# Spectral filter, expert layer and MLP in one kernel: first and last transform in pairs of chunks, x before the other loads, constant tables on SyncE's queue

## The chip, the cores and the metric

One core of a Trainium2 chip runs the whole program. The metric is the device time of one execution in microseconds (us). A difference counts here as one over 0.2% of the time before, 6.7 us.

## The reference

```python
X = np.fft.rfft(x, axis=1)                       # x: 8 x 3072 x 256
Yr = X.real @ w_r - X.imag @ w_i + b_r
Yi = X.real @ w_i + X.imag @ w_r + b_i
Y  = shrink(Yr, 0.01) + 1j * shrink(Yi, 0.01)    # soft threshold
x  = np.fft.irfft(Y, n=3072, axis=1).reshape(24576, 256)
# 8 experts, the best one per token, tokens with x @ w_skip > 0 only
out = x;  out[t] += gate[t] * relu(x[t] @ w1[e]) @ w2[e]
h = out @ w_in
y = (max(h, 0) + alpha * min(h, 0)) @ w_out      # d_ff = 2048
```

## The kernel before, in words

The 3072-point transform of a batch is split in two. Token index and frequency are cut as 3072 = 48 x 64, so the work of one batch b (of 8) has four stages.

- **A** (`A_load` L163, `A_mm` L179, `A_store` L184): the 48-point part, over all 64 residues m. A residue is (j, q) with j in 0, 1 and q in 0..31. The 32 q are cut into 8 *chunks* of 4. A chunk is loaded by two DMAs (one for each j) to an `xin` tile of 48 partitions twice, each partition getting 4 rows of 256 numbers, 4 KB in one run. `quarters` (L169) does eight matmuls, ScalarE copies one half out of PSUM and VectorE the other (L177), and two DMAs store the tile `sa` to the DRAM scratch `sA`.
- **B and C** (`S_load`, `B_mm`, `mix`, `gather`, `shrink`, `C_mm`, `C_store`): the 64-point part, by 24 residue classes taken in 12 pairs `pp`. `S_load` fetches six classes (three pairs) from `sA`; it needs all chunks of the batch stored. `B_mm` multiplies by the class matrices `fct` (L215, L235), `mix` applies the weights (L292 for pair 0, L263 for the others), `C_mm` turns back with the matrices `cct` (L330, L324), and ScalarE copies the result to a tile `zc` (L331, L325, L326), of which there are two. `C_store` (L335) writes it to the scratch `sZ`.
- **D** (`D_load` L339, `D_mm` L345, `D_store` L350): the 48-point part backwards, again in 8 chunks: `zin` in, `xo` out, and the rows of the filtered tokens go to the DRAM buffer `xb`, 2 rows (2 KB) to a run. `T_tr` transposes `xo` for the router.
- Then routing, expert jobs and the MLP (L882 to L1067), which read `xb`.

The order is written by hand. A loop over steps s = 12 b + pp (L707) does in each step: stores that are due (`store`, the `zc` store first), x loads for the chunks of step s + 2 (`a_need`), D loads for step s + 2 (`d_need`), every third step an `S_load`, then `B_mm` of the next pair, `mix`, a D chunk, `C_mm` of the pair before, and the A chunks of the step. `a_at` (L573) says how many half chunks (units u) of A a step gets: two (one chunk) up to step 14 and in the steps with s % 12 in 0, 1, 2, 11; one in the others. So batch b + 1 goes through A while batch b goes through B and C.

Before the loop, batch 0 goes through A alone: 8 chunks, `setup0` (L630, it makes the weight tables `wri` on VectorE) after the sixth. Then the first `S_load`, cut into three DMAs of two classes, and B starts (L215).

Nearly all DMAs are issued by SyncE (SP in the profile) in program order: an instruction that waits keeps everything behind it waiting. The 8 tables `fct` and `cct` (six classes each) are issued by GpSimd, and in batch 0 the second half of each A store by ScalarE. The framework gives SP's and ScalarE's DMAs eight completion semaphores in turn, so a DMA also waits until the last one on its own semaphore has landed.

Of the kernel before, what the change touches and what calls it, by code (L numbers as in the profile page):

```python
# [10 lines left out]
F32 = mybir.dt.float32  # L11
# [9 lines left out]
B, SEQ, D = 8, 3072, 256  # L21
NT = B * SEQ
NQ, NP = 32, 96
NC = 24
# [18 lines left out]
CP = 6  # L43
# [4 lines left out]
def _constants():  # L48
    A, G = np.zeros((2, 64, 64)), np.zeros((2, 64, 64))
    n1 = np.arange(48)  # L50
    for c in range(NC):
        ang = 2 * np.pi * ((n1 * c) % 48) / 48
        for ri in range(2):
            if c == 0:
                f = g = np.ones(48) if ri == 0 else (-1.0) ** n1
            else:
                f = np.cos(ang) if ri == 0 else -np.sin(ang)
                g = 2 * f
            A[:, :48, 2 * c + ri] = f
            G[:, 2 * c + ri, :48] = g / SEQ  # L60
    Fm, Cm = np.zeros((NC, 128, 128)), np.zeros((NC, 128, 128))
    n2 = np.arange(64)
    for c in range(NC):
        for f in range(64):
            if c:
                k = c + 48 * f
                rows, sg, mul = None, (1 if f < 32 else -1), 1
            else:
                k = 24 * (f // 32) + 48 * (f % 32)
                rows, sg, mul = slice(64 * (f // 32), 64 * (f // 32) + 64), 1, 2  # L70
            ang = 2 * np.pi * ((n2 * k) % SEQ) / SEQ
            co, si = np.cos(ang), np.sin(ang)
            if c:
                Fm[c, :64, f], Fm[c, 64:, f] = co, si
                Fm[c, :64, 64 + f], Fm[c, 64:, 64 + f] = -si * sg, co * sg
                Cm[c, f, :64], Cm[c, f, 64:] = co, si
                Cm[c, 64 + f, :64], Cm[c, 64 + f, 64:] = -si * sg, co * sg
            else:
                Fm[0, rows, f], Fm[0, rows, 64 + f] = co, -si
                Cm[0, f, rows], Cm[0, 64 + f, rows] = mul * co, -mul * si  # L80
                if f == 0:
                    Fm[0, rows, 64] = np.cos(np.pi * n2)
                    Cm[0, 0, rows] = 1.0
                    Cm[0, 64, rows] = np.cos(np.pi * n2)
    m = np.arange(64)
    m = 32 * (m // 2 % 2) + 4 * (m // 8) + 2 * (m // 4 % 2) + m % 2
# [9 lines left out]
    q = 16 * (r // 12) + 4 * g + 2 * (c // 48 % 2) + c // 96 % 2  # L96
# [12 lines left out]
def spectral_moe_mlp(ctx, tc, x, w_r, w_i, b_r, b_i, w_skip, w_gate, w1, w2,  # L109
# [28 lines left out]
    if True:  # L138
# [21 lines left out]
        turn = [pa]  # L160
        xin, sast = {}, {}

        def A_load(b, ch):  # L163
            t = xin[b, ch] = p2.tile([128, 4, D], F32, name="xin", bufs=6)
            for j in range(2):
                nc.sync.dma_start(t[64 * j:64 * j + 48],
                                  x[b].rearrange("(n j q) d -> j n q d", j=2, q=NQ)[j, :, 4 * ch:4 * ch + 4])

        def quarters(k, t, o):  # L169

            q = [bank(turn[0]), bank(turn[0])]
            for h in range(2):
                for j in range(2):
                    nc.tensor.matmul(q[j][64 * h:64 * h + 64], agt[64 * j:64 * j + 48, k],  # L174
                                     t[64 * j:64 * j + 48, 2 * h:2 * h + 2, :], start=True, stop=True)
            for j in range(2):
                (nc.vector.tensor_copy if j > k else nc.scalar.copy)(o[:, j], q[j].rearrange("p (a d) -> p a d", d=D))  # L177

        def A_mm(b, ch):  # L179
            t = p2.tile([128, 2, 2, D], F32, name="sa", bufs=3)  # L180
            quarters(0, xin[b, ch], t)
            stores.append(lambda: A_store(b, ch, t))

        def A_store(b, ch, t):  # L184
            for h in range(2):
                eng = nc.scalar if b == 0 and h else nc.sync
                eng.dma_start(sA[b % 3].rearrange("c r m d -> (c r) m d")[:, 8 * ch + 4 * h:8 * ch + 4 * h + 4],
                              t[64 * h:64 * h + 48].rearrange("p j a d -> p (j a) d"))

        stores = []  # L190

# [144 lines left out]

        zin, xo, sal = {}, {}, {}

        def D_load(b, ch):  # L339
            t = zin[b, ch] = t2.tile([128, 4, D], F32, name="zin", bufs=3)  # L340
            for j in range(2):
                nc.sync.dma_start(t[64 * j:64 * j + 48],
                                  sZ[b % 3].rearrange("c r j q d -> j (c r) q d")[j, :, 4 * ch:4 * ch + 4])

        def D_mm(b, ch):  # L345
            t = xo[b, ch] = t2.tile([128, 2, 2, D], F32, name="xo", bufs=4)
            quarters(1, zin[b, ch], t)
            stores.append(lambda: D_store(b, ch, t))

        def D_store(b, ch, t):  # L350
            v = xb[X0 + SEQ * b:X0 + SEQ * b + SEQ].rearrange("(n j q) d -> n j q d", j=2, q=NQ)
            for h in range(2):
                nc.sync.dma_start(v[:, :, 4 * ch + 2 * h:4 * ch + 2 * h + 2], t[64 * h:64 * h + 48])

        xt = {}

        def T_tr(b, ch, kt):
            src = xo[b, ch]
# [213 lines left out]
        d_rest += [(B - 1, u) for u in range(16)]  # L572
        k, s = 0, 0  # L573
        while k < 16 * (B - 1):
            n = 2 if s < 15 or s % 12 in (0, 1, 2, 11) else 1
            a_at[s] = [(1 + i // 16, i % 16) for i in range(k, min(k + n, 16 * (B - 1)))]
            k, s = k + n, s + 1

        a_loaded, d_loaded = set(), set()

        def a_need(b, u):
            if (b, u // 2) not in a_loaded:
                a_loaded.add((b, u // 2))
                A_load(b, u // 2)

        def d_need(b, u):
            if (b, u // 2) not in d_loaded:
                d_loaded.add((b, u // 2))
                D_load(b, u // 2)


        q_tr, q_mm, routing, routed = [], [], [], [0]
# [81 lines left out]
        consts = [(t, a, p) for q in range(NC // CP + 1) for t, a, p in ((fct, fc, q), (cct, cc, q - 1)) if 0 <= p < NC // CP]  # L674

        def const_load(n):

            for t, a, p in consts[:n]:
                nc.gpsimd.dma_start(t[:, CP * p:CP * p + CP], a[:, CP * p:CP * p + CP])
            del consts[:n]  # L680

        nc.scalar.dma_start(agt, ag)
        wst = p2.tile([128, 4, 2, D], F32, name="wst", bufs=1)
        for k, w in ((0, w_r), (3, w_i)):
            nc.scalar.dma_start(wst[:, k], w.rearrange("(k p) d -> p k d", p=128))
        for u in range(0, 12, 2):
            a_need(0, u)
        for i in range(16):
            if i in (4, 6):
                a_need(0, i + 8)  # L690
            if i == 4:
                const_load(1)
            if i % 2 == 1:
                A_mm(0, i // 2)
            if i % 2 == 1 and i > 1:
                store()
            if i == 12:
                setup0()
        for k in a_at[0] + a_at[1]:
            a_need(*k)  # L700
        store()
        S_load(0, 0)
        S_load(0, 1)
        bias_load()
        const_load(2)
        B_mm(0, 0)
        for s in range(NS + 1):  # L707
            b, pp = bp(s)
# [680 lines left out]
```

## Time and profile before

| | us |
|---|---|
| median of 3 runs (3338.28 to 3339.12) | 3338.47 |
| the profiled execution | 3341.88 |
| its span on the core | 3340.2 |
| TensorE (PE) busy in it | 3252.1 (97%) |
| the DMA engines' mean busy share, first 500 us | about 0.9 |

How to read it: times in the rows are us from the span's start. A line L174 is line 174 of the kernel before; PE is the matmul engine, DVE VectorE, ACT ScalarE, POOL GpSimd, SPq the DMA issues of SyncE. The chain is the work that ended last, followed backwards from the end: a piece "DMA S<-sA" is time in which everything later hung on that transfer. PEclk is the granted TensorE clock as a share of full speed.

### The profile page before, as it was taken

The numbers are of one execution on the slowest core, as the hardware profiler recorded it, in microseconds if no ns is written. First come the engines' busy times: TensorE is split into PE (matmuls) and PEld (weight loads), VectorE is DVE, ScalarE is ACT, GpSimd is POOL, SyncE is SP. The second block draws the span as 40 slices with busy tenths as digits, with TensorE's granted clock in tenths as the row PEclk, the third lists the DMA queues.
The fourth block names the chain that finished last, engine by engine and source line by source line (L and its number), as shares of the span: only waits on it lengthen the run. The fifth ranks groups of instructions, "written<-read, shape, count | busy, mean of one in ns | idle before, by whom it ended". The sixth has DMA issues, their size and how long they took to land.

```text
span 3340.2 us, 51269 instructions
## 1 busy us (share of the span) xinstructions
PE 3252.1 (97%) x17606; PEld 2599.8 (78%) x17606; DVE 2328.4 (70%) x3681; ACT 2026.4 (61%) x4050; POOL 1869.7 (56%) x1566
## 2 busy tenths in 40 slices
PE   7999999899999999999999999999999999999998
PEld 4777777677888887888888888888888888888886
DVE  4566666546676666777777777777777777777775
ACT  3556555443344434777777777777777777777775
POOL 2236666737565654555555555555555555555554
PEclk9999999999999999999999999999999999999999
DMA  8989997643332222111111111111111111111100
GB/s 240 276 260 246 247 253 206 161 128 86 89 119 91 91 75 66 25 24 25 26 26 26 26 26 26 26 26 26 26 26 26 26 26 25 23 25 22 26 12 18
DMA packets 361398, 269.01 MB, mean 81 GB/s; under 512 B 242397, under 2 KB 321631, under 8 KB 361126
## 3 DMA queue, kind: packets, MB, share of 16 engines
q1 hardware_dynamic: 341526, 234.13, 26.9%
q0 software_dynamic: 16288, 28.82, 2.9%
q10 hardware_dynamic: 3312, 2.69, 0.3%
q8 instruction: 140, 2.29, 0.3%
q14 instruction: 132, 1.08, 0.1%
HBM read 149.65 MB, written 116.47 MB: 80 GB/s over the span
## 4 chain that ended last, share of the span: by engine, by line
PE 88%; DVE 3%; POOL 3%; DMA 3%; issue 2%; ACT 1%; SPq 1%; ACTq 0%; DVEq 0%; POOLq 0%
PE bank L1057 32%; PE bank L1005 28%; PE bank L882 6%; PE bank L263 5%; PE bank L901 4%; PE bank L174 3%; PE bank L235 2%; PE bank L902 2%; PE bank L324 2%; PE bank L363 1%; POOL lst L498 1%; DMA wraw<-in_moe_w 1%; PE bank L376 1%; PE bank L292 1%; DMA sA<-sa 1%
## 5 line engine op out<-in xcount | busy, mean ns | idle before, releaser
L1046 POOL TENSOR_TENSOR gl<-P,gh 128x512 fp32r<-128x512 f32 x768 | 1046.5, 1377 | 839.0 <-ACT gh L1045 721.1
L1005 PE MATMUL bank<-wex,wi 128*128 128x512 f32 x4032 | 1009.3, 397 | 5.3 <-ACT u L1016 2.7
L1057 PE MATMUL bank<-gh,wo 128*128 128x512 f32 x3072 | 965.9, 395 | 0.0
L1005 PEld LDWEIGHTS bank<-wex,wi 128*128 128x128 f32 x4032 | 752.9, 188 | 199.6 <-DVE C L1018 8.3
L1057 PEld LDWEIGHTS bank<-gh,wo 128*128 128x128 f32 x3072 | 577.0, 188 | 139.6 <-issue 0.2
L1038 DVE SCALAR_TENSOR_TENSOR P<-R,al,P 128x512 f32<-128x512 f32 x768 | 567.1, 756 | 117.9 <-ACT R L1037 114.9
L1057 PE MATMUL bank<-gl,wo 128*128 128x512 f32 x1536 | 607.4, 395 | 0.0
L1045 ACT CAST gh<-P 128x512 fp32r<-128x512 f32 x768 | 454.6, 617 | 237.7 <-PE bank L1057 237.7
L1028 DVE TENSOR_TENSOR C<-bank,u 128x512 f32<-128x512 f32 x384 | 262.0, 689 | 206.1 <-PE bank L1005 204.8
L1036 ACT ACTIVATE P<-C 128x512 f32<-128x512 f32 x576 | 358.2, 622 | 53.5 <-DVE C L1028 50.7
L1037 ACT ACTIVATE R<-C 128x512 f32<-128x512 f32 x576 | 355.8, 618 | 0.0
L1057 PEld LDWEIGHTS bank<-gl,wo 128*128 128x128 f32 x1536 | 288.5, 188 | 69.8
L901 PE MATMUL bank<-wex,gh 128*128 128x512 f32 x792 | 294.5, 402 | 19.7 <-DVE os L920 12.8
L886 DVE SCALAR_TENSOR_TENSOR gl<-bank,gh 128x512 fp32r<-128x512 f32 (+2 forms) x232 | 141.5, 610 | 204.7 <-ACT gh L885 203.8
L882 PE MATMUL bank<-xTh,wex 128*128 128x512 f32 (+2 forms) x928 | 269.2, 372 | 6.2 <-DVE gl L886 2.1
L885 ACT ACTIVATE gh<-bank 128x512 fp32r<-128x512 f32 (+2 forms) x232 | 124.3, 537 | 248.1 <-PE bank L882 245.4
L1036 ACT ACTIVATE P<-bank 128x512 f32<-128x512 f32 x192 | 114.9, 598 | 238.7 <-PE bank L1005 237.4
L498 POOL DMA_INDIRECT lst<-pay,di x192 | 199.3, 1038 | 53.7 <-issue 47.9
L902 PE MATMUL bank<-wex,gl 128*128 128x256 f32 x792 | 224.7, 284 | 3.7 <-DVE gl L886 3.7
L269 POOL TENSOR_TENSOR ub<-u,biasj 128x512 f32<-128x512 f32 x88 | 113.0, 1284 | 199.9 <-DVE m L243 113.3
L263 PE MATMUL bank<-wri,m 128*128 128x256 f32 x1584 | 214.8, 290 | 8.7 <-ACT zc L326 4.8
L263 PEld LDWEIGHTS bank<-wri,m 128*128 128x128 f32 x1584 | 198.0, 193 | 10.3 <-ACT zc L326 5.4
(180 smaller groups left out, 4384.1 us busy)
## 6 DMA issues: line engine op xcount, KB each, us to landing
xin<-in_x SPq DMA_DIRECT2D x128, 192.0 KB
sZ<-zc SPq DMA_DIRECT2D x96, 256.0 KB
zin<-sZ SPq DMA_DIRECT2D x128, 192.0 KB
xb<-xo SPq DMA_DIRECT2D x128, 192.0 KB
xr<-xb SPq DMA_DIRECT2D x192, 128.0 KB
out<-os SPq DMA_DIRECT2D x188, 128.0 KB
S<-sA SPq DMA_DIRECT2D x31, 768.0 KB
sA<-sa SPq DMA_DIRECT2D x120, 192.0 KB
```

What stands on the lines that cost most here:

```text
L263: nc.tensor.matmul(o, m[:, kt, xa, j], wri[:, wa, w, kt], start=(n == 0), stop=(n == 5))
L882: nc.tensor.matmul(q, a, b[:, kt, :N], start=(i == 0), stop=(i == 5))
L901: nc.tensor.matmul(o, gh[:, 128 * a:128 * a + 128], w, start=(f == 0), stop=False)
L902: nc.tensor.matmul(o[:, 0:256], gl[:, 128 * a:128 * a + 128], w[:, 0:256], start=False, stop=(f == NFE - 1))
L1005: nc.tensor.matmul(o[:, :n], w[:, k, m], b, start=(first and i == 0), stop=(i == 2), skip_group_check=True)
L1028: V.tensor_tensor(out=C[:, i], in0=q[2 + i][:, :n], in1=u, op=add)
L1036: nc.scalar.activation(g, src, AF.Relu)
L1037: nc.scalar.activation(R, src, AF.Relu, scale=-1.0)
L1038: V.scalar_tensor_tensor(out=g, in0=R, scalar=mlp['al'][:, 2 * c + f:2 * c + f + 1], in1=g, op0=mult, op1=add)
L1045: nc.scalar.copy(gh[:, :n], P[f][:, t, :n])
L1046: nc.gpsimd.tensor_tensor(out=gl[:, :n], in0=P[f][:, t, :n], in1=gh[:, :n], op=sub)
L1057: nc.tensor.matmul(oacc[j][t][h], w[:, k, 128 * h:128 * h + 128], b, start=(f + i == 0), stop=(f == NF - 1 and i == 2))
```

## The change

- Chunks are loaded, stored and kept in pairs. A DMA of `xin`, `sA`, `zin` and `xb` carries two chunks, 384 KB in place of 192 KB, and there are half as many. In SBUF the two chunks of a partition lie 64 bytes apart (`half`), so that a run stays 4 KB. The runs to `xb` become 4 KB (2 KB before). `m` and `q` in the constants, and so the order of the residues, follow.
- An A or D chunk's load is due when the first chunk of its pair is; its store goes out after the second.
- Buffers: `xin` 3 pairs (6 chunks before), `sa` 2 pairs (3 chunks), `zin` 2 pairs (3 chunks), `xo` 2 pairs (4 chunks). Batch 0 uses two free `zin` tiles for `sa`, so that none of its four pairs waits for a store; `wst` moves to an `xo` tile.
- Batch 0: x loads stand ahead of the weights in the program, all A stores are issued by SyncE.
- The tables are issued by SyncE, one at a time: `fct` 0 behind x, `cct` 0 and `fct` 1 around the first `S_load`, the rest one in each step with s % 3 > 0.
- `a_at`: one chunk in each step up to step 8 (14 before).

```diff
-            t = xin[b, ch] = p2.tile([128, 4, D], F32, name="xin", bufs=6)
+            t = xin[b, pr] = half(p2.tile([128, 2, 4 * D + 16], F32, name="xin", bufs=3))
...
         def A_mm(b, ch):
-            t = p2.tile([128, 2, 2, D], F32, name="sa", bufs=3)
-            quarters(0, xin[b, ch], t)
-            stores.append(lambda: A_store(b, ch, t))
+            pr, c = divmod(ch, 2)
+            if c == 0:
+                pool, tag = (t2, "zin") if b == 0 and pr % 3 == 0 else (p2, "sa")
+                sast[b, pr] = half(pool.tile([128, 2, 4 * D + 16], F32, name="sa", tag=tag))
+            t = sast[b, pr]
+            quarters(0, xin[b, pr], c, [t[:, c, 512 * j:512 * j + 512] for j in range(2)])
+            if c:
+                stores.append(lambda: A_store(b, pr, t))
...
-                eng = nc.scalar if b == 0 and h else nc.sync
...
-            n = 2 if s < 15 or s % 12 in (0, 1, 2, 11) else 1
+            n = 2 if s < 9 or s % 12 in (0, 1, 2, 11) else 1
...
-                nc.gpsimd.dma_start(t[:, CP * p:CP * p + CP], a[:, CP * p:CP * p + CP])
+                nc.sync.dma_start(t[:, CP * p:CP * p + CP], a[:, CP * p:CP * p + CP])
...
         nc.scalar.dma_start(agt, ag)
-        wst = p2.tile([128, 4, 2, D], F32, name="wst", bufs=1)
+        wst = t2.tile([128, 4, 2, D], F32, name="wst", tag="xo")
+        for pr in range(3):
+            a_need(0, 4 * pr)
         for k, w in ((0, w_r), (3, w_i)):
             nc.scalar.dma_start(wst[:, k], w.rearrange("(k p) d -> p k d", p=128))
-        for u in range(0, 12, 2):
-            a_need(0, u)
...
+        for ch in range(8):
+            A_mm(0, ch)
+            if ch == 1:
+                a_need(0, 12)
                 const_load(1)
+            store()
+            if ch == 5:
                 setup0()
         for k in a_at[0] + a_at[1]:
             a_need(*k)
-        store()
+        const_load(1)
         S_load(0, 0)
         S_load(0, 1)
+        const_load(1)
         bias_load()
-        const_load(2)
...
-            if s % 3 == 0:
-                const_load(2)
             store()
+            if s % 3:
+                const_load(1)
```

The class matrices and x and scratch rows carry the same numbers as before, and TensorE's matmuls are the same in kind and number; apart from some A chunks that come up to two steps later from step 9 on, their order is the same too.

SyncE's queue at the start, before (`xin` is x, `sA` the A stores; the names in brackets are what the DMA waits for, DMAHW0 to 7 the eight completion semaphores):

```order
L166 DMA xin<-in_x 48x1024 x5
L166 DMA xin<-in_x 48x1024 [waits DMAHW0_49]
L166 DMA xin<-in_x 48x1024 [waits DMAHW1_49]
L166 DMA xin<-in_x 48x1024 [waits DMAHW3_49]
L166 DMA xin<-in_x 48x1024 [waits DMAHW5_49]
L166 DMA xin<-in_x 48x1024 [waits DMAHW7_49]
L166 DMA xin<-in_x 48x1024 [waits DMAHW0_49]
L166 DMA xin<-in_x 48x1024 [waits DMAHW1_49]
L187 DMA sA_59<-sa 48x1024 [waits DMAHW2_49,DVE_49,Activation_49]
```

The same place, changed (L170 is the x load, L692 a table, L195 the A store):

```order
L170 DMA xin<-in_x 48x2x1024 x5
L170 DMA xin<-in_x 48x2x1024 [waits DMAHW0_49]
L170 DMA xin<-in_x 48x2x1024 [waits DMAHW4_49,DMAHW1_49,PE_49]
L170 DMA xin<-in_x 48x2x1024 [waits DMAHW2_49]
L692 DMA fct<-const_fc 128x768 [waits DMAHW3_49]
L195 DMA sA_59<-sa 48x2x1024 [waits DVE_49,Activation_49]
L195 DMA sA_59<-sa 48x2x1024 [waits DMAHW5_49]
```

Before, twelve DMAs stand ahead of the first store and the eighth waits for a semaphore that a weight load holds; now all of batch 0's x is in eight DMAs, and the table `fct` stands between them and the first store.

SyncE's queue around the first `S_load` of batch 1, steps 7 to 9, before (L335 is the `zc` store, L672 the fill of the token list, L203 the `S_load`):

```order
L335 DMA sZ_62<-zc 128x2x256
L187 DMA sA_60<-sa 48x1024 x2
L166 DMA xin<-in_x 48x1024 x2
L203 DMA S<-sA_60 128x6x256
L672 DMA lst<-pad 128x294 x4
L335 DMA sZ_62<-zc 128x2x256
```

And changed:

```order
L343 DMA sZ_62<-zc 128x2x256
L195 DMA sA_60<-sa 48x2x1024 x2
L211 DMA S<-sA_60 128x6x256
L685 DMA lst<-pad 128x294 x4
L343 DMA sZ_62<-zc 128x2x256
L170 DMA xin<-in_x 48x2x1024 x2
```

The x load that stood between the last A store of the batch and the `S_load` has gone behind the next `zc` store, and the A store is twice as large.

SyncE's queue in steps 16 to 18, where all stages run, before:

```order
L335 DMA sZ_63<-zc 128x2x256
L353 DMA xb<-xo 96x1x512 x2
L342 DMA zin<-sZ_62 48x1024 x2
L335 DMA sZ_63<-zc 128x2x256
L353 DMA xb<-xo 96x1x512 x2
L187 DMA sA_61<-sa 48x1024 x2
L166 DMA xin<-in_x 48x1024 x2
L342 DMA zin<-sZ_62 48x1024 x2
L203 DMA S<-sA_60 128x6x256
```

And changed (L365 is the store to `xb`, L350 the load of `zin`):

```order
L343 DMA sZ_63<-zc 128x2x256 x2
L365 DMA xb<-xo 96x1x1024 x2
L170 DMA xin<-in_x 48x2x1024 x2
L350 DMA zin<-sZ_62 48x2x1024 x2
L211 DMA S<-sA_60 128x6x256
L343 DMA sZ_63<-zc 128x2x256 x2
```

One step now issues nothing but its `zc` store, and the next 3.4 MB.

## Rows read from the trace of the kernel before

**Rows 1.** The page: busy tenths of PE and DMA in 40 slices of 83.5 us.
```profile
PE   7999999899999999999999999999999999999998
...
DMA  8989997643332222111111111111111111111100
```
**Rows 2.** Windows: stretch, length, busy of PE, PEld, DVE, ACT, POOL, PEclk, DMA share, GB/s.
```profile
0.00:40.00 40.00, 22.65 (x64) 4.89 (x64) 10.20 (x13) 5.97 (x9) 3.59 (x11) 1.00 0.89 233
40.00:80.00 40.00, 35.77 (x302) 28.83 (x303) 22.71 (x44) 17.48 (x42) 11.74 (x13) 1.00 0.86 240
80.00:120.00 40.00, 35.34 (x326) 27.55 (x328) 23.85 (x45) 16.90 (x43) 12.67 (x14) 0.91 0.97 277
...
120.00:500.00 380.00, 380.00 (x3666) 286.15 (x3659) 235.88 (x486) 223.07 (x556) 195.96 (x194) 1.00 0.91 255
```
**Rows 3.** The chain, 36 to 60 us: start, length, what.
```profile
35.30 3.93 DMA sA<-sa
...
39.29 4.81 DMA S<-sA
...
44.23 2.05 PE bank L215 x8
```
**Rows 4.** SyncE's own waits, 0 to 60 us: us in total, times, longest.
```profile
SPq L166 <- DMA wst<-in_w_i: 10.7, 1, 10.7
```
**Rows 5.** The timeline, 27 to 46 us: start, length, engine.
```profile
33.47 1.28 DVE L177 COPY sa<-bank 128x512 f32<-128x512 f32 x2
...
35.69 3.05 SPq L166 DMA_DIRECT2D xin<-in_x  x4
```
**Rows 6.** The page's DMA issues: KB of each DMA.
```profile
lst<-pad SPq DMA_DIRECT2D x16, 147.0 KB
...
fct<-const_fc POOLq DMA_DIRECT2D x4, 384.0 KB
```
**Rows 7.** Windows of the first A stage and of two short stretches.
```profile
4.00:32.00 28.00, 22.65 (x64) 4.89 (x64) 7.45 (x11) 4.10 (x7) 0.84 (x2) 1.00 1.00 265
...
32.00:36.00 4.00, 0.00 (x0) 0.00 (x0) 2.75 (x3) 0.59 (x1) 0.00 (x0) 1.00 0.44 84
...
52.00:56.00 4.00, 4.00 (x36) 3.52 (x29) 3.04 (x6) 2.13 (x5) 1.08 (x1) 1.00 0.36 95
...
108.00:112.00 4.00, 2.48 (x11) 2.48 (x12) 0.83 (x2) 2.42 (x6) 0.00 (x0) 0.50 1.04 291
```
**Rows 8.** The timeline: `zc` stores and copies, and the `S_load` of batch 1.
```profile
57.28 0.39 SPq L335 DMA_DIRECT2D sZ<-zc  x1
...
98.98 0.39 SPq L203 DMA_DIRECT2D S<-sA  x1
99.42 2.07 SPq L672 DMA_DIRECT2D lst<-pad  x4
101.53 0.48 SPq L335 DMA_DIRECT2D sZ<-zc  x1
...
108.82 0.37 ACT L325 COPY zc<-bank 128x256 f32<-128x256 f32 x1 [7.27 <-DMA sZ<-zc]
```
**Rows 9.** The chain, 96 to 120 us.
```profile
101.53 7.21 DMA sZ<-zc
...
109.52 4.21 PE bank L263 x18
...
116.86 2.87 PE bank L292 x24
```
**Rows 10.** The chain, 0 to 1500 us: the first `mix` of batch 2.
```profile
191.87 2.87 PE bank L292 x24
```
**Rows 11.** Waits of all engines, 120 to 500 us: `zc` copies for a DMA.
```profile
ACT zc L325 <- DMA sA<-sa: 3.1, 3, 1.4
```
**Rows 12.** The timeline, 575 to 760 us: SyncE's four stores to `xb`.
```profile
647.35 3.05 SPq L353 DMA_DIRECT2D xb<-xo  x4
```
**Rows 13.** The chain, 640 to 670 us: the wait for the expert weights.
```profile
653.27 9.32 DMA wraw<-in_moe_w
```

More of the change, by code (lines that the diff above doesn't have):

```diff
@@ L85, in _constants @@
     m = np.arange(64)
-    m = 32 * (m // 2 % 2) + 4 * (m // 8) + 2 * (m // 4 % 2) + m % 2
+    m = 32 * (m // 2 % 2) + 8 * (m // 16) + 4 * (m // 8 % 2) + 2 * (m // 4 % 2) + m % 2
     Fm = Fm[:, np.concatenate([m, 64 + m])]
@@ L95, in _constants @@
     c = 32 * (r % 12) + i
-    q = 16 * (r // 12) + 4 * g + 2 * (c // 48 % 2) + c // 96 % 2
+    q = 16 * (r // 12) + 8 * (g // 2) + 4 * (c // 48 % 2) + 2 * (g % 2) + c // 96 % 2
     tok = (X0 + SEQ * b + 64 * (c % 48) + 32 * (c // 192) + q).astype(np.float32)
@@ L161, in spectral_moe_mlp, with half, A_load, quarters @@
         xin, sast = {}, {}
-        def A_load(b, ch):
-            t = xin[b, ch] = p2.tile([128, 4, D], F32, name="xin", bufs=6)
+        def half(t):
+            return t[:, :, 0:4 * D]
+        def A_load(b, pr):
+            t = xin[b, pr] = half(p2.tile([128, 2, 4 * D + 16], F32, name="xin", bufs=3))
             for j in range(2):
                 nc.sync.dma_start(t[64 * j:64 * j + 48],
-                                  x[b].rearrange("(n j q) d -> j n q d", j=2, q=NQ)[j, :, 4 * ch:4 * ch + 4])
-        def quarters(k, t, o):
+                                  x[b].rearrange("(n j g q) d -> j n g (q d)", j=2, g=8, q=4)[j, :, 2 * pr:2 * pr + 2])
+        def quarters(k, t, c, o):
             q = [bank(turn[0]), bank(turn[0])]
@@ L174, in quarters, with A_store @@
                     nc.tensor.matmul(q[j][64 * h:64 * h + 64], agt[64 * j:64 * j + 48, k],
-                                     t[64 * j:64 * j + 48, 2 * h:2 * h + 2, :], start=True, stop=True)
+                                     t[64 * j:64 * j + 48, h, 2 * D * c:2 * D * c + 2 * D], start=True, stop=True)
             for j in range(2):
-                (nc.vector.tensor_copy if j > k else nc.scalar.copy)(o[:, j], q[j].rearrange("p (a d) -> p a d", d=D))
+                (nc.vector.tensor_copy if j > k else nc.scalar.copy)(o[j], q[j])
         def A_mm(b, ch):
-            t = p2.tile([128, 2, 2, D], F32, name="sa", bufs=3)
-            quarters(0, xin[b, ch], t)
-            stores.append(lambda: A_store(b, ch, t))
-        def A_store(b, ch, t):
+            pr, c = divmod(ch, 2)
[6 more added lines that the diff above has]
+                stores.append(lambda: A_store(b, pr, t))
+        def A_store(b, pr, t):
             for h in range(2):
-                eng = nc.scalar if b == 0 and h else nc.sync
-                eng.dma_start(sA[b % 3].rearrange("c r m d -> (c r) m d")[:, 8 * ch + 4 * h:8 * ch + 4 * h + 4],
-                              t[64 * h:64 * h + 48].rearrange("p j a d -> p (j a) d"))
+                nc.sync.dma_start(sA[b % 3].rearrange("c r (g m) d -> (c r) g (m d)", m=4)[:, 4 * pr + 2 * h:4 * pr + 2 * h + 2],
+                              t[64 * h:64 * h + 48])
         stores = []
@@ L337, in spectral_moe_mlp, with D_load, D_store @@
         zin, xo, sal = {}, {}, {}
-        def D_load(b, ch):
-            t = zin[b, ch] = t2.tile([128, 4, D], F32, name="zin", bufs=3)
+        def D_load(b, pr):
+            t = zin[b, pr] = half(t2.tile([128, 2, 4 * D + 16], F32, name="zin"))
             for j in range(2):
                 nc.sync.dma_start(t[64 * j:64 * j + 48],
-                                  sZ[b % 3].rearrange("c r j q d -> j (c r) q d")[j, :, 4 * ch:4 * ch + 4])
+                                  sZ[b % 3].rearrange("c r j (g q) d -> j (c r) g (q d)", q=4)[j, :, 2 * pr:2 * pr + 2])
         def D_mm(b, ch):
[L346 to L350, printed above, removed]
+            pr, c = divmod(ch, 2)
+            if c == 0:
+                xo[b, pr] = t2.tile([128, 2, 2, 2, D], F32, name="xo")
+            t = xo[b, pr]
+            quarters(1, zin[b, pr], c, [t[:, j, c].rearrange("p a d -> p (a d)") for j in range(2)])
+            if c:
+                stores.append(lambda: D_store(b, pr, t))
+        def D_store(b, pr, t):
             v = xb[X0 + SEQ * b:X0 + SEQ * b + SEQ].rearrange("(n j q) d -> n j q d", j=2, q=NQ)
             for h in range(2):
-                nc.sync.dma_start(v[:, :, 4 * ch + 2 * h:4 * ch + 2 * h + 2], t[64 * h:64 * h + 48])
+                nc.sync.dma_start(v[:, :, 8 * pr + 4 * h:8 * pr + 4 * h + 4],
+                                  t[64 * h:64 * h + 48].rearrange("p j c a d -> p j (c a) d"))
         xt = {}
         def T_tr(b, ch, kt):
-            src = xo[b, ch]
+            src = xo[b, ch // 2][:, :, ch % 2]
             if kt == 0:
@@ L581, in a_need @@
         def a_need(b, u):
-            if (b, u // 2) not in a_loaded:
-                a_loaded.add((b, u // 2))
-                A_load(b, u // 2)
+            if (b, u // 4) not in a_loaded:
+                a_loaded.add((b, u // 4))
+                A_load(b, u // 4)
         def d_need(b, u):
-            if (b, u // 2) not in d_loaded:
-                d_loaded.add((b, u // 2))
-                D_load(b, u // 2)
+            if (b, u // 4) not in d_loaded:
+                d_loaded.add((b, u // 4))
+                D_load(b, u // 4)
         q_tr, q_mm, routing, routed = [], [], [], [0]
@@ L672, in fill_list @@
             nc.sync.dma_start(lst.rearrange("(g p c) k -> g p c k", g=16, p=128)[i], padt[0])
-        consts = [(t, a, p) for q in range(NC // CP + 1) for t, a, p in ((fct, fc, q), (cct, cc, q - 1)) if 0 <= p < NC // CP]
+        consts = [(t, a, p) for q in range(NC // CP + 1) for t, a, p in ((cct, cc, q - 1), (fct, fc, q)) if 0 <= p < NC // CP]
         def const_load(n):
             for t, a, p in consts[:n]:
-                nc.gpsimd.dma_start(t[:, CP * p:CP * p + CP], a[:, CP * p:CP * p + CP])
+                nc.sync.dma_start(t[:, CP * p:CP * p + CP], a[:, CP * p:CP * p + CP])
             del consts[:n]
         nc.scalar.dma_start(agt, ag)
-        wst = p2.tile([128, 4, 2, D], F32, name="wst", bufs=1)
+        wst = t2.tile([128, 4, 2, D], F32, name="wst", tag="xo")
+        for pr in range(3):
+            a_need(0, 4 * pr)
         for k, w in ((0, w_r), (3, w_i)):
             nc.scalar.dma_start(wst[:, k], w.rearrange("(k p) d -> p k d", p=128))
-        for u in range(0, 12, 2):
-            a_need(0, u)
[L688 to L691, printed above, removed]
-                const_load(1)
-            if i % 2 == 1:
-                A_mm(0, i // 2)
-            if i % 2 == 1 and i > 1:
-                store()
-            if i == 12:
+        for ch in range(8):
+            A_mm(0, ch)
+            if ch == 1:
+                a_need(0, 12)
+                const_load(1)
+            store()
+            if ch == 5:
                 setup0()
@@ L700, in spectral_moe_mlp @@
             a_need(*k)
-        store()
+        const_load(1)
         S_load(0, 0)
         S_load(0, 1)
+        const_load(1)
         bias_load()
-        const_load(2)
         B_mm(0, 0)
```

## The prediction

> **What bounds the kernel now.** I read the page first: TensorE's busy tenths show 9 nearly everywhere, with 7 in the first slice, and the DMA engines are full in the first sixth only [rows 1]. The windows then split that sixth: TensorE misses 17.4 us of the first 40, 4.2 of the next and 4.7 of the third, and from 120 to 500 us it misses nothing, although the DMA share there is 0.91 [rows 2]. So matmuls set the time from 120 us on; a faster or slower DMA can be seen ahead of that, or later where it makes TensorE wait.
>
> The chain names the two places ahead of 120 us. The first is the start: the last A store of batch 0 is issued at 35.30 and lands 3.93 later, the first load of `S` takes 4.81 more, and B starts at 44.23 [rows 3]. Behind that last store stands SyncE, which waited 10.7 us for a weight load while x was due [rows 4], and VectorE, which came to its last two copies only at 33.47, after `setup0` [rows 5]; the DMA engines ran dry meanwhile, 0.44 busy from 32 to 36 us [rows 7]. The second is at 101.53: ScalarE waits 7.27 us for a `zc` store issued at 101.53, and TensorE goes on at 109.52, at half its clock at first: granted 0.50 [rows 7 to 9]. It went so because SyncE's queue was late: the store was issued behind A stores, an `S` load and the list fills [rows 8].
>
> **The change, part by part.** The sum is made against the profiled execution, 3341.88 us, which is 3.41 above the median of the runs.
>
> *Start.* Matmuls are the same. What must pass through the DMA engines before B can start is, changed: x of batch 0 3072 KB, `agt` 64, weights 512, one `fct` 384 [rows 6], A stores 3072, the next x pair 768, `cct` 384 and the first third of `S` 256, together 8512 KB or 8.72 MB. Before, the four other tables that GpSimd issued at once took their share too. At the 265 GB/s of the first A stage [rows 7] that is 32.9 us; with about 2 us until bytes move (my estimate: the first issue at 0.81 and its way) it ends at 34.9. To that comes the landing. The first `S` load with the four x loads ahead of it, 1.05 MB, took 4.81 for 4.0 at that rate, 0.8 more; the last A store, 0.2 MB, took 3.93 for 0.7, 3.2 more [rows 3, 5]. I take 3.1, since `S` waits for such a store: B starts at **38.0** in place of 44.23, a gain of 6.2. Lower end: the chain alone. Pairs of x have landed by 16, `setup0` follows the sixth chunk and the last store is issued at 25 to 26 by my estimate; 8.93 us from there (44.23 - 35.30 [rows 3]) give 34.5. Upper end: `fct` 0 waits on SyncE for the semaphore of a weight load, and the A stores stand behind it. If it lands as late as now, the last store is 3 us earlier than before only and B starts at 41.
>
> [...]
>
> *Second place.* From the first `zc` store (57.28 [rows 8], 13.05 after B's start) until the eighth has landed, the queues carry, in KB: before, eight `zc` stores 2048, A stores 2688, x 2688, `S` 2304, list fills 1764 (12 of 147 [rows 6]), tables 1152, small loads 257: 13.21 MB in 51.46 us, 257 GB/s. Changed: 2048, 3072, 2304, 2304, 1764, 1536 and 257: 13.60 MB. The tables that left the start come back here; the one chunk a step from step 9 saves nothing before that store. The first `zc` store goes out at 38.0 + 13.05 = 51.05, and nothing is queued up there: 11.96 MB have to have passed, which at 265 takes until 47.1. Rate: 257 at the low end, 277 at the high end, the window with the fullest engines [rows 2]; I take 265, nearer to the one measured with the same waits. 13.60 MB take 51.3 us, until 102.4. The `S` load of batch 1 now stands right behind the A store that it waits for; before, 384 KB of x ran meanwhile, worth 1.5 us at that rate. I take 1.0 (0 to 1.5) for it: 103.4 for 108.74 [rows 8], a gain of **5.3** (257: 3.8; 277: 7.6). The wait remains, about as long as now, and so does the half clock behind it: nothing more is gained there. So the start's 6.2 are not all kept.
>
> *From 116 to 540 us.* A step lasts 6.25 us (116.86 to 191.87 over 12 steps [rows 9, 10]) and TensorE is full: the larger runs to `xb`, fewer DMAs and eight table issues less on GpSimd lie beside it, 0. What is lost if that cover goes is the third rival. A chunks that come up to two steps later move matmuls, not their sum: 0; their `S` loads come a step or more later still.
>
> *Tail.* At 647.35 SyncE issues four stores to `xb` in 3.05 us, then the expert weights, and the chain waits 9.32 for them [rows 12, 13]. Two stores in place of four save half the issue, 1.5 us; the `zin` pair between the two weight loads has 384 KB more, which costs 1.5 at 265. I take 0, between -1.5 and 1.5.
>
> Sum: 3341.88 - 5.3 = 3336.6 for a profiled execution, **3333.2** against the median.
>
> **The rivals.**
> *Both waits shrink.* If the larger DMAs run faster, the byte bound goes below the pace of the steps. The start then gives 6.2 to 9.7, the wait at 101.53 up to 5.9 of its 7.27 (about 1.4 of ScalarE's idle time there is TensorE's own pace, an estimate), and the half clock 2.1 (L263 takes 4.21, twice its length at full clock [rows 7, 9]): 8 to 17 us, 14 in the middle, 3324.5. For it: rates from 233 to 277 at shares of 0.9 to 0.97 [rows 2], so busy engines are not all at one pace; SyncE also issues half as many. Against it: the runs of x and `sA` were 4 KB already.
> [...]
> *Given back.* The start gains, but the second stretch is bound by bytes and by SyncE's order, with 0.39 MB more: at 257, with the full 1.5 and B at 41, the gain is 0 to 1, 3338. The change then doesn't do at the start what it says. For it: the share there is 0.97 already [rows 2].
> *Bursts.* Steps now alternate: 0.26 MB, then 3.41 MB (`zc` store, x, `zin`, `xb` or A store, `S`), where the largest was 2.62. SyncE's queue is in order, so the next `zc` store waits behind the burst. It is issued a step after the burst began and must have landed two steps after that, 18.75 from the start; with 3.2 us of landing, 3.67 MB have 15.5 us: from 237 GB/s downward ScalarE waits for it and TensorE with it. The mean is 255 [rows 2], and such waits are 3.1 us in all now [rows 11]. Ten such steps (16, 22, 28, ... 70) at 2 us each are 20 lost: 3353; at 1 us 3343.
>
> **How the numbers follow.** The forecast, a gain of 2 to 8 us, has 0.47; both waits shrinking 0.27; given back 0.13; bursts 0.13. The range goes from 3324 (the middle of the first rival) to 3342 (the bursts at their mildest), and leaves out some 0.06 below and 0.11 above. What a measurement can tell from no change is 6.7 us. Faster by more: 0.27 and the upper part of the forecast, 0.13, together 0.40. Slower by more than that: most of the bursts, 0.09. Within: 0.51.
>
> **What would show it.** B's first matmul (L215 before) at 38, with 34.5 to 41 as the ends; the wait for a `zc` store still there near 97 to 103, and the first `mix` of batch 1 about 5 us ahead of 116.86. From there to 500 us TensorE at 100%, and ScalarE's waits for `zc` not above a few us. If the `zc` wait has gone, the first rival holds; if TensorE misses time between 116 and 540, the third; if B starts early and `mix` of batch 1 does not, the second. The forecast is wrong if the time is above 3342 or below 3324.

## The result, and the profile after

The change makes the kernel slower: 3368.24 us median (3362.89 to 3373.0) beside 3338.38 us (3333.04 to 3339.12) for the kernel before, a ratio of 1.0097 with an interval of 1.0085 to 1.0109, some 30 us. The prediction was 3333.2, in a range that ended at 3342.

The profiled execution of the changed kernel took 3362.89 us, its span 3361.0; TensorE is busy for 3257.7 us (97%). It is 21 us above the profiled execution of before. The medians are 30 apart: this profile comes from the lowest of the four runs, that of before from 3.5 above its median. The page hardly shows the loss; TensorE and DMA in 40 slices, as in [rows 1]:

```profile
PE   7999999889999999999999999999999999999998
...
DMA  9999998662333222011111111111111111111101
```

The windows show it. Beside [rows 2] the first 120 us are no better, and from 120 to 500 us, where TensorE missed nothing, it now misses 8.75 us at a mean granted clock of 0.98:

```profile
0.00:40.00 40.00, 20.18 (x64) 4.57 (x64) 10.28 (x13) 5.98 (x9) 0.70 (x6) 1.00 0.94 212
40.00:80.00 40.00, 37.41 (x316) 30.10 (x320) 23.81 (x50) 17.80 (x44) 11.19 (x13) 1.00 0.91 242
80.00:120.00 40.00, 33.45 (x293) 26.04 (x294) 21.89 (x37) 15.39 (x40) 10.95 (x12) 0.87 0.98 273
120.00:500.00 380.00, 371.25 (x3463) 275.03 (x3462) 223.25 (x456) 211.25 (x527) 181.37 (x181) 0.98 0.93 242
```

**The start.** Lines of the kernel after are 4 to 13 higher up to L400 or so (B's first matmul is L223, the D and A matmuls L178, the first `mix` of a batch L300). The chain, 0 to 60 us, beside [rows 3]:

```profile
5.93 13.30 DMA xin<-in_x
...
25.27 1.24 DVE wri L649
26.53 2.29 DVE wri L650
28.82 1.21 DVE sa L181 x2
...
30.43 5.44 DMA sA<-sa
...
36.02 5.69 DMA S<-sA
...
41.84 2.04 PE bank L223 x8
```

B starts at 41.84 in place of 44.23, 2.4 us earlier. The chain now hangs on x itself, then on `setup0` (the `wri` tables), behind which VectorE makes the last copies. And x is slow. The window of 4 to 18 us, about four fifths of it x (most of the rest the weights), with engines full:

```profile
4.00:18.00 14.00, 10.68 (x33) 2.52 (x34) 2.07 (x3) 1.76 (x3) 0.00 (x0) 1.00 1.06 186
```

That is 186 GB/s, where the first stage of before had 265 [rows 7].

**The second place.** The chain from 60 to 600 us, beside [rows 9, 10]:

```profile
102.49 7.40 DMA sZ<-zc
...
117.93 2.84 PE bank L300 x24
...
194.81 2.84 PE bank L300 x24
```

The same wait for a `zc` store is there, and the first `mix` of batch 1 comes 1.07 us after its time before: the start's gain is gone. Batch 1 then takes 76.88 us (117.93 to 194.81) where it took 75.01.

**From 116 us on.** The two pieces of the chain ahead of the second transform (D) of batch 4, which runs beside batch 5, and the first `mix` of batches 5 and 6:

```profile
432.73 2.84 PE bank L300 x24
...
437.31 8.65 DMA sZ<-zc
...
446.01 7.08 DMA zin<-sZ
...
453.13 2.64 PE bank L178 x3
...
514.35 2.84 PE bank L300 x24
```

Batch 5 takes 81.62 us; before it was 75.15. SyncE's timeline (start, length, line) there:

```profile
429.81 3.20 SPq L170 DMA_DIRECT2D xin<-in_x  x2
433.11 0.38 SPq L211 DMA_DIRECT2D S<-sA  x1
433.59 4.07 SPq L343 DMA_DIRECT2D sZ<-zc  x2
438.34 0.79 SPq L195 DMA_DIRECT2D sA<-sa  x2
439.23 4.00 SPq L170 DMA_DIRECT2D xin<-in_x  x2
446.01 0.79 SPq L350 DMA_DIRECT2D zin<-sZ  x2
```

The last `zc` store of batch 4, the second of the two at 433.59, is issued at 437.31. In the 7.5 us ahead of it an x pair, an `S` load and a `zc` store were issued, 1.8 MB; right behind it follow `sA` stores and the next x pair, 1.5 MB. The `zin` pair needs that store landed, which it has after 8.65 us, and lands itself 7.08 later. TensorE has run out of work by then. The waits of TensorE, 100 to 560 us, and the windows around 453:

```profile
PE bank L178 <- DMA zin<-sZ: 10.7, 8, 2.2
```
```profile
452.00:454.00 2.00, 0.87 (x1) 0.28 (x2) 0.49 (x1) 0.00 (x0) 1.99 (x3) 0.74 1.05 278
454.00:456.00 2.00, 2.00 (x11) 0.56 (x13) 1.32 (x3) 0.00 (x0) 1.53 (x3) 0.50 1.09 375
456.00:458.00 2.00, 2.00 (x18) 0.94 (x13) 0.00 (x0) 0.91 (x2) 1.70 (x2) 0.50 1.24 174
458.00:460.00 2.00, 2.00 (x13) 1.32 (x8) 0.00 (x0) 0.81 (x3) 0.08 (x1) 0.56 1.02 198
```

It waits 2.2 us, and comes back at a granted clock of 0.50 until nearly 460. Over the whole batch both parts can be read off one window, first of after, then of before:

```profile
432.73:514.35 81.62, 79.41 (x727) 58.05 (x726) 47.82 (x101) 44.26 (x110) 46.56 (x47) 0.96 0.93 233
```
```profile
417.35:492.50 75.15, 75.15 (x726) 56.57 (x726) 47.48 (x101) 44.14 (x110) 46.77 (x47) 1.00 0.93 254
```

Idle 2.21 us, and the same matmuls 4.26 us longer (79.41 - 75.15): together the 6.47 us that the batch lost. The half clock is not all of the 4.26: the 6.6 us at 0.50, from 453.13 to 459.75, are worth 3.3 at most (an estimate, at twice the time for the same work: the 18 matmuls of L271 took 4.21 us at 0.50, from 110.67, and 2.14 at 1.00, from 425.90). The rest, some 1 us or more, falls beside a second wait. The weight loads of these matmuls (PEld) wait for `zin` twice, the second time, by their order, for the other half of the partitions, and TensorE counts as busy then (2.00 us of 2.00 from 454 to 456); PEld's waits, 432 to 515 us:

```profile
PEld bank L178 <- DMA zin<-sZ: 4.1, 2, 2.4
```

The DMA share is the same 0.93 over a longer time, at 233 GB/s for 254. By 514.35, where before had 492.50, 21.9 us are lost, and by the first `mix` of batch 7 26.1 (595.62 for 569.50).

**The tail.** The wait for the expert weights, beside [rows 13], is 2.2 us longer and ends at 690.41 for 662.59:

```profile
678.88 11.53 DMA wraw<-in_moe_w
```

### The profile page after: what moved, and what is told of

Its sections match the earlier page's. It is cut to its first block, busy times and chain, and to the rows that moved or that the text cites. A ratio compares the mean times of both kernels' runs of the same rounds, so it can differ in the third digit from the quotient of the medians.

```text
span 3361.0 us, 50826 instructions
## 1 busy us (share of the span) xinstructions
PE 3257.7 (97%) x17606; PEld 2601.5 (77%) x17606; DVE 2330.3 (69%) x3681; ACT 2026.4 (60%) x4050; POOL 1862.7 (55%) x1558
## 3 DMA queue, kind: packets, MB, share of 16 engines
q14 instruction: 127, 1.04, 0.1%
## 4 chain that ended last, share of the span: by engine, by line
PE 87%; DMA 5%; DVE 2%; POOL 2%; issue 1%; ACT 1%; SPq 1%; DVEq 0%; ACTq 0%; POOLq 0%
PE bank L1067 32%; PE bank L1015 28%; PE bank L892 7%; PE bank L911 4%; PE bank L271 4%; PE bank L178 3%; PE bank L912 2%; PE bank L332 2%; PE bank L243 2%; DMA sZ<-zc 2%; DMA zin<-sZ 1%; PE bank L376 1%; DMA wraw<-in_moe_w 1%; PE bank L300 1%; PE bank L389 1%
## 5 line engine op out<-in xcount | busy, mean ns | idle before, releaser
L271 PE MATMUL bank<-wri,m 128*128 128x256 f32 x1584 | 215.0, 290 | 13.1 <-ACT zc L334 9.2
L271 PEld LDWEIGHTS bank<-wri,m 128*128 128x128 f32 x1584 | 197.7, 192 | 15.6 <-ACT zc L334 10.5
```

The source lines that it names most:

```text
L271: nc.tensor.matmul(o, m[:, kt, xa, j], wri[:, wa, w, kt], start=(n == 0), stop=(n == 5))
```

## The experiments

Two theories. **Order**: in each batch the first `zin` pair stands on SyncE behind the landing of the last `zc` store and comes too late for a fixed step; a matter of when it is due. **Rate**: the pair loads hold the DMA engines longer than the single chunks did, so everything behind them is late. The second has rivals of its own: the size of one DMA, the length of a run, or which partitions the queue holds at a time. Each kernel's ratio is to the kernel before on the same chip in the same session; e5 to e8 ran on a chip where that took 3395.87 us, the others where it took 3332.87 to 3333.59. In the first 500 us times compare all the same: an undisturbed batch takes 75.2 us there too (75.15 in e7_dpair, 75.16 in e8_best).

**e1_dlater**, the second transform one step later.

```diff
-                st = 12 * (b + 1) + 3 + u // 2
+                st = 12 * (b + 1) + 4 + u // 2
```

> Every D unit one step later (st = 12 (b + 1) + 4 + u // 2), all else as changed, so the first zin load of a batch is due a step after the last zc store. Theory 1 (order: the first zin pair waits on SyncE for the last zc store of its batch and lands 2 us late, and TensorE then runs at half clock): the waits of L178 for zin go, batches 3 to 6 are 75 to 76 us apart in place of 80 to 82, time 3340 to 3346. Theory 2 (rate: the large loads keep the DMA engines busy some 75 us per batch in place of 70): the lateness comes back at another wait, batches stay at 78 or more, time above 3352. B still starts at 41.8 by both.

Measured: 3344.48 us, ratio 1.0029 (1.0017 to 1.0040). The waits for `zin` are gone between 100 and 560 us and the clock is at 1.00 from 200 to 600. So the deadline is where the loss arose: 7 of the 10 thousandths come back with every byte as it was. But the engines are now full from 200 to 500 us, at 249 GB/s, where before moved 252 at a share of 0.92:

```profile
200.00:500.00 300.00, 297.21 (x2870) 222.85 (x2872) 189.12 (x396) 176.05 (x439) 169.37 (x169) 1.00 0.99 249
```

That the same traffic takes 0.99 in place of 0.92 is for the second theory. A batch takes 76.1 us; the 0.9 us of idle time in it are waits for VectorE and GpSimd, the price of the other order.

**e2_dsingle**, the changed kernel with the second transform in single chunks again (loads of 192 KB, `xo` stores of 192 KB); with less room left, `sa` has two tiles in all.

```diff
-                pool, tag = (t2, "zin") if b == 0 and pr % 3 == 0 else (p2, "sa")
+                pool, tag = (p2, "sa")
...
-            t = zin[b, pr] = half(t2.tile([128, 2, 4 * D + 16], F32, name="zin"))
+            t = zin[b, ch] = t2.tile([128, 4, D], F32, name="zin", tag="zin1", bufs=3)
```

> D in single chunks as before the change (192 KB loads, 2 KB runs to xb, three zin and four xo tiles), A and the start as changed. Theory 1: the first zin load has half the bytes, lands 1.5 us or more earlier, little or no wait: batches 75 to 76, time 3340 to 3346. Theory 2: half of the slow loads are back to the old size, DMA busy time per batch near 72, batches 76 to 78, time 3346 to 3356.

Measured: 3346.22 us, 1.0039 (1.0027 to 1.0052). TensorE is busy for all of 200 to 500 us and a batch takes 74.9 to 75.4 us, as before. What its trace shows of a loss lies ahead of that: with two `sa` tiles batch 0's pairs wait for their stores, B starts at 46.65 and the first `mix` of batch 1 at 123.57, 5.6 us behind the changed kernel's and 6.7 behind that of before. The other half of the 13 us that the median lost can't be seen in this trace, whose execution (3339.98) was the fastest of six. So pairs of x and `sA` alone cost nothing from 124 us on; it takes the `zin` pairs.

**e3_tworings**, half of batch 0's first x pairs issued by ScalarE.

```diff
+                eng = nc.scalar if b == 0 and pr < 3 and j else nc.sync
-                nc.sync.dma_start(t[64 * j:64 * j + 48],
+                eng.dma_start(t[64 * j:64 * j + 48],
```

> Batch 0's second-half x loads (partitions 64 to 111) of the first three pairs are issued by ScalarE, so that both halves of the partitions are loaded at once. If x is slow because a 384 KB load fills one half of the partitions at a time: rate from 4 to 16 us above 260 GB/s where it is 185 to 190, B starts at 36 to 39. If it is slow because its DRAM rows lie 64 KB apart: the rate stays below 210 and B starts at 41 to 43. The rest stays as changed: 3358 to 3370.

Measured: 3363.11 us, 1.0091 (1.0074 to 1.0107), no different from the change. x did come faster, 212 GB/s from 4 to 18 us where the changed kernel has 186, though less than was expected, and A's matmuls were done before 26. B still started at 41.62: the last copies and the last A store (29.82, changed 30.43) stood behind `setup0` on VectorE, whose second table ran until 28.2. `setup0` in turn stands behind the sixth chunk, whose copy came only 0.6 us earlier (22.51 for 23.13).

**e4_headonly**, the kernel before with all of the change but the pairs: order of the first loads, A stores on SyncE, tables on SyncE, `a_at`.

```diff
-            n = 2 if s < 15 or s % 12 in (0, 1, 2, 11) else 1
+            n = 2 if s < 9 or s % 12 in (0, 1, 2, 11) else 1
...
-                nc.gpsimd.dma_start(t[:, CP * p:CP * p + CP], a[:, CP * p:CP * p + CP])
+                nc.sync.dma_start(t[:, CP * p:CP * p + CP], a[:, CP * p:CP * p + CP])
```

> The kernel before with all edits but the pairs: x ahead, tables one at a time on SyncE, all A stores on SyncE, one chunk a step from step 9; chunks single, 192 KB. Theory 1 and 2: TensorE full from 120 to 500 us, batches 75.2 apart. If large loads are what slows x: B starts at 37 to 40 and the time is 3333 to 3337. If x alone is slow at either size: B starts at 41 to 44, time 3336 to 3340.

Measured: 3332.68 us, 0.9996 (0.9986 to 1.0005), no change. B starts at 41.50, the first `mix` of batch 1 at 115.90 (116.86 before), batches take 75.0 to 75.2. So the whole loss is the pairs', and the new order of the loads gains 1 us at that point, where the whole change was forecast to gain 5.3. The wait for `zc` stores stays: 16.6 us on ScalarE from 60 to 125.

**e5_split**, the changed kernel with every load of x and `zin` cut in four, the halves of the partitions in turn.

```diff
-            for j in range(2):
-                nc.sync.dma_start(t[64 * j:64 * j + 48],
-                                  x[b].rearrange("(n j g q) d -> j n g (q d)", j=2, g=8, q=4)[j, :, 2 * pr:2 * pr + 2])
+            for g in range(2):
+                for j in range(2):
+                    nc.sync.dma_start(t[64 * j:64 * j + 48, g],
+                                      x[b].rearrange("(n j g q) d -> j n g (q d)", j=2, g=8, q=4)[j, :, 2 * pr + g])
```

> The changed kernel, but every load of a pair of x or zin chunks is issued as four DMAs of 192 KB, the two halves of the partitions in turn, in place of two of 384 KB. Tiles, order and waits of whole pairs stay. Theory 1 (order: the first zin pair of a batch stands on SyncE behind the landing of the last zc store, with 768 KB of x ahead of that): nothing there changes, batches stay near 81 us apart, 3364 to 3372 us. Theory 2 (rate: one DMA of 384 KB into 48 partitions holds the DMA engines longer than two of 192 KB): x at the start goes from about 185 GB/s to 200 or more as in e4_headonly, the DMA share of 200 to 500 us falls, batches come down to 76 to 77 us, 3342 to 3350 us.

Measured: 1.0024 (1.0014 to 1.0034). No wait for `zin` is left in the list of 100 to 600 us, although order and due times are those of the change. The rate theory holds too, then. From 200 to 500 us:

```profile
200.00:500.00 300.00, 299.12 (x2842) 222.64 (x2841) 184.74 (x385) 173.61 (x431) 169.72 (x168) 1.00 0.90 245
```

But batches still take 75.3 to 77.8 us: some waiting is left inside TensorE's busy time. The D matmuls of the batch from 340.87 (77.80 us, at a clock of 1.00), then of one batch of before (busy us, mean ns, idle us ahead):

```profile
L179 PE MATMUL bank<-zin,agt 48*64 48x512 f32 x64 | 11.2, 614 | 0.1
```
```profile
L174 PE MATMUL bank<-zin,agt 48*64 48x512 f32 x64 | 8.7, 614 | 0.0
```

And the start changes: the sixth chunk's copy comes at 18.84, and B, with `setup0` where it was, starts 4.5 us ahead of the changed kernel:

```profile
37.35 2.09 PE bank L224 x8
```

**e6_dfirst**, `zin` ahead of x in each step.

```diff
-            for k in a_at.get(s + 2, []):
-                a_need(*k)
             for k in d_at.get(s + 2, []):
                 d_need(*k)
+            for k in a_at.get(s + 2, []):
+                a_need(*k)
```

> The changed kernel, but in each step the zin loads are issued ahead of the x loads. Theory 1, with the x pair as the culprit: the last zc store of a batch has no x pair beside it and lands in 4 to 5 us in place of 8.65, the zin pair is issued about 4 us earlier, TensorE's waits for zin (10.7 us) and the half clock behind them go, 3343 to 3350 us. Theory 1, with the pair of zin chunks itself as the culprit: little gained, 3360 us. Theory 2 (rate): the same bytes at the same rate, 3358 to 3368 us.

Measured: 1.0059 (1.0043 to 1.0074): a miss, between the cases. The waits for `zin` go, but others come. SyncE now stands at the `zin` issue until the `zc` store has landed (19.1 us in six waits from 100 to 560 us, 5.4 in three in the changed kernel), and everything behind it moves back, the next `zc` stores among it (the chain has one of 10.91 us, from 441.28). Of TensorE's waits, 100 to 560 us, the longest in total is now this one, 3.7 us in the changed kernel:

```profile
PE bank L271 <- ACT zc L334: 11.3, 6, 3.2
```

**e7_dpair**, e4_headonly with the second transform alone in pairs.

```diff
-            t = zin[b, ch] = t2.tile([128, 4, D], F32, name="zin", bufs=3)
+            t = zin[b, pr] = half(t2.tile([128, 2, 4 * D + 16], F32, name="zin"))
```

> e4_headonly with the second transform alone in pairs (zin loads of 384 KB, xo stores of pairs); the first transform in single chunks. If the pair of zin chunks alone makes TensorE wait: first matmul of a zin pair waits 1 to 2 us in each batch and half clock follows, batches near 80 us, 3355 to 3365 us. If it needs the x pair in the queue ahead of it: no wait, 75.2 to 76 us a batch, 3333 to 3340 us. I take the second, 3338 us.

Measured: 1.0010 (1.0001 to 1.0020). One wait of 0.5 us for `zin` is left from 100 to 560 us. With e2_dsingle: pairs in one of the two transforms are nearly free there, pairs in both are not. The `zin` pair makes TensorE wait more than that only with x pairs in the queue.

**e8_best**, e4_headonly with two waits of the profile taken away: `setup0` after the eighth chunk, and the list fills (`fill_list`, 2.4 MB) later.

```diff
-            if ch == 5:
+            if ch == 7:
                 setup0()
...
-            for i in range(4 * (s - 7), 4 * (s - 6)):
+            for i in range(2 * (s - 12), 2 * (s - 11)):
```

> A version meant to beat both kernels: e4_headonly with setup0 after the last chunk of the first stage in place of the sixth, and the list fills two a step from step 12 in place of four a step from step 7. If VectorE's setup0 holds the last A stores, B starts at 38 to 39.5 in place of 41.50. If the wait for a zc store near 102 us is made of bytes, it goes with 1.76 MB of list fills, first mix of batch 1 at 108 to 112 in place of 115.90; 3324 to 3330 us. If the wait is one of order only, it stays, and 3332 us comes out.

Measured: 0.9962 (0.9948 to 0.9977), faster than both kernels. B starts at 37.36, the first `mix` of batch 1 is at 102.48 (115.90 in e4_headonly). TensorE misses nothing from 60 to 120 us; before it missed 4.66 there, and ran at a clock of 0.94:

```profile
60.00:120.00 60.00, 60.00 (x570) 46.67 (x563) 42.36 (x81) 31.68 (x79) 20.39 (x23) 1.00 0.93 283
```

**e9_split_same**, e5_split with the two loads of one half in a row.

```diff
-            for g in range(2):
-                for j in range(2):
+            for j in range(2):
+                for g in range(2):
```

> e5_split with its four DMAs of 192 KB in the other order: both for one half of the partitions first, then both for the other half. Theory 2a (a load is slow while the queue holds one half of the partitions only): the two in a row act as one of 384 KB, x at the start at 175 to 195 GB/s, batches near 81 us, 1.007 to 1.010 of before. Theory 2b (what counts is the size of one DMA): as e5_split, x at 200 to 230 GB/s, batches 76 to 78 us, 1.001 to 1.004.

Measured: 3359.28 us, 1.0076 (1.0059 to 1.0093). Number, size and bytes of the DMAs are those of e5_split; only their order differs, and by the two ratios, which are from two chips, 5 of its 7.6 thousandths of loss come from that. The wait for `zin` is back:

```profile
PE bank L179 <- DMA zin<-sZ: 5.4, 8, 1.2
```

The rate of x in the window 10 to 18 us, of e9_split_same, then of the next kernel, which loads as e5_split does:

```profile
10.00:18.00 8.00, 7.64 (x28) 2.31 (x28) 2.07 (x3) 2.00 (x4) 0.00 (x0) 1.00 1.03 163
```
```profile
10.00:18.00 8.00, 8.00 (x43) 2.72 (x40) 3.21 (x5) 2.63 (x6) 0.00 (x0) 1.00 1.04 232
```

163 against 232 GB/s, with the engines full in both. In the same window the changed kernel has 183, e5_split 225, e4_headonly (192 KB, halves in turn) 203.

**e10_split_dlater**, e5_split and e1_dlater together (both diffs above).

> e5_split and e1_dlater together: loads in alternating quarters, and the second transform one step later. If rate and deadline make up the whole loss, batches are at 75.0 to 75.5 us, TensorE waits for nothing from 200 to 500 us, and the time is that of before, 0.998 to 1.001. If pairs cost something else besides (stores of pairs, the issue on SyncE), 1.002 to 1.004 stays.

Measured: 3335.05 us, 1.0008 (0.9998 to 1.0017): the loss is gone. A batch takes 76.2 us as in e1_dlater, so the expected 75.0 to 75.5 is missed (the order's price stays), but at a DMA share of 0.92 for 0.99: loading the halves in turn alone freed 7% of the engines' time. It comes to the time of before since batch 1's first `mix` is at 112.85, 4 us earlier: B starts at 37.93, beside 41.38 in e9_split_same on the same chip.

**e11_nogap**, the changed kernel without the gap between the chunks of a tile.

```diff
-            t = xin[b, pr] = half(p2.tile([128, 2, 4 * D + 16], F32, name="xin", bufs=3))
+            t = xin[b, pr] = half(p2.tile([128, 2, 4 * D], F32, name="xin", bufs=3))
```

> The changed kernel without the 64 B gap between the two chunks of a tile, so that one partition's run can be 8 KB in place of twice 4 KB. [...] If only which partitions are loaded counts, nothing moves: 1.008 to 1.011 of before.

Measured: 3365.22 us, 1.0099 (1.0082 to 1.0116), as the change. x ran at 202 GB/s in the window 10 to 18, above the 183 with the gap; the time does not show it. The gap is not what costs.

**e12_pairs_best**, e10_split_dlater with the two edits of e8_best.

> e10_split_dlater (pairs, loads in alternating quarters, second transform one step later) with the two edits of e8_best: setup0 after the last chunk of the first stage, list fills two a step from step 12. If pairs cost nothing once their loads alternate and have time, these edits give what they gave without pairs (some 13 us at the first mix of batch 1, 0.4% of the time): first mix of batch 1 at 100 to 104 in place of 112.85, ratio to before 0.996 to 0.998. If pairs hold the queue longer so that the wait for a zc store stays, 0.999 to 1.001.

Measured: 3323.27 us, 0.9970 (0.9961 to 0.9979). First `mix` of batch 1 at 102.29. The edits gain with pairs what they gain without, and pairs add nothing to e8_best.

## Why the prediction was wrong

**The step "from 116 to 540 us ... lie beside it, 0"** failed, and it is most of the error. I read that TensorE was full there and costed every larger transfer at nothing. The cover was thin at one place that I did not look up: the first `zin` load of a batch, issued 8.2 us after the next batch's first `mix` before (425.51 for 417.35) and 13.3 after it now. It is needed 18.2 us after that `mix` in both: before it had 10 us to land, now 4.9, and it took 7.08. TensorE lost 2.2 us idle, then 4.3 in matmuls at half clock with a second wait among them, 6.5 in this batch; by 514 us 21.9 in all. The third rival had the mechanism, a burst on SyncE's queue that makes a `zc` store land late. It named the wrong victim: ScalarE's wait for a free `zc` tile, in ten steps at up to 2 us. That is 7.9 us in four places from 120 to 500 us, and TensorE's list there has no wait behind it. TensorE waited instead for the load that needs the same store, mostly once a batch, and in the batch above lost three times its idle time. Its threshold, 237 GB/s, lies between the 242 of 120 to 500 us and the 233 of the batch above, which says little: 233 is about the 254 of before spread over the longer batch. e1_dlater shows the deadline and e5_split the late transfer: either alone takes away most of the loss, so neither is "the" cause; it takes both.

**The step "at the 265 GB/s of the first A stage"** failed. Those 265 were x mixed with tables of 128 partitions and with stores [rows 7]. With x put ahead of all, in DMAs of 384 KB for one half of the partitions and then the other, the rate was 186. The chain alone gave 34.5 and the bytes 38.0; it was 41.84, above the upper end of 41, with 212 GB/s in the mean of the first 40 us. The gap between 163 and 232 GB/s (e9_split_same, e10_split_dlater) shows what the rate hung on there: whether the halves alternate in the queue; the size of a DMA is the same in both, and alternating brought 42%. From 10 to 18 us the three kernels that load one half and then the other ran at 163 to 202 (e9_split_same 163, the change 183, e11_nogap 202), five of the six with 192 KB in turn at 225 to 267 (e5_split 225, e10_split_dlater 232, e12_pairs_best 243, and, with a table among the loads, e8_best 253 and e7_dpair 267). The sixth, e4_headonly, had 203, hardly more than e11_nogap. Why halves in turn go faster, no run here shows.

There was a second reason at the start: `setup0` held the last copies. Where it comes after the eighth chunk, B starts at 37.36 (e8_best) and 35.88 (e12_pairs_best); where it does not, at 40.09 (e7_dpair, on the chip of e8_best) and 37.93 (e10_split_dlater). My sum had let only bytes and landings count, although `setup0` stood in [rows 5]. The order of the loads is worth more than that, 3.5 us (37.93 for the 41.38 of e9_split_same): with it alone and `setup0` where it was, e5_split and e10_split_dlater start B at the 38.0 that I had forecast and reach the first `mix` of batch 1 at 112.54 and 112.85, 4 us ahead of before, most of the 5.3 that I had counted.

**The second place** was sized rightly in kind and wrongly in sum. The wait stayed, as forecast, and its bytes moved at 267 GB/s between 60 and 120 us, for which I had taken 265. With B at 41.84 my own sum (13.05 us to the first store, 51.3 for the bytes, 1.0 more) ends at 107.2; the wait ended at 109.9. So 3.8 of the 5.3 us that I counted were lost with the start, and 2.7 us more in this stretch, for a reason that no run separates. That this wait is made of bytes is borne out by e8_best, where the list fills come later and TensorE has no wait from 60 to 125 us (ScalarE waits 4.2 us for `zc` stores there, 16.6 in e4_headonly); `setup0` moved there too, so how much each of the two gave was not separated.

**The tail**, 0 (between -1.5 and 1.5), was 2.2 on the weight load, just outside. In all the changed kernel is 27.8 us late there, 26.1 of them from ahead of batch 7.

Of the rivals, "both waits shrink" rested on larger DMAs running faster; they ran slower (x at 183 GB/s from 10 to 18 us, beside 203 in e4_headonly). "Given back" describes the first 117 us closely: 1.07 us lost, for a gain of 0 to 1. The chance of slower, 0.09, was too small because the one mechanism on that side was priced by its idle time without the slower work behind it.

## What to carry to other kernels

A stretch in which the busiest engine is full hides a slower transfer only as far as the nearest load that feeds it has slack (here the first `zin` pair had 4.9 us and took 7.08): for each load that gets larger, look up in the timeline what it waits for and how long it lies ready before it is needed. A short wait of TensorE can cost more than its length: here the granted clock was 0.50 for 6.6 us after it, and a batch lost 6.5 us where the engine was idle for 2.2. And load a tile whose partitions lie in two halves in small alternating pieces, not one half and then the other (here 232 GB/s for x against 163).

## What the runs showed of the hardware that was not expected

Four loads of 192 KB into two halves of 48 partitions run at 163 GB/s in the order 1, 1, 2, 2 and at 232 in the order 1, 2, 1, 2, with the DMA engines' share at 1.03 and 1.04: full engines are not engines at their best rate. In the steady stretch, the same change of the loads brought the share from 0.99 to 0.92 at equal pace. A wait of TensorE of 2.2 us was followed by 6.6 us at a granted clock of 0.50; with a second wait among them, of 1.7 us by the weight loads, the work took 4.3 us longer.
